# Linear attention with an MLP behind it: the products of queries with states move to the head of the next unit, and gated queries get two places

## The chip, the cores and the metric

The kernel runs on one core of a Trainium2 chip, all tensors in 32-bit floats. The metric is the device time of one execution in microseconds. Five runs of the kernel before took 703.0 to 706.71 us, with a median of 704.47. The execution that was profiled took 703.88 us.

## The reference

Four sequences of 768 tokens, with 8 heads of 48 channels. Each head carries a 48 x 48 state that is decayed by a gate f and grown by an outer product, and every token's query reads it. The result, as 3072 rows of 384 channels, goes through an MLP with 2048 hidden channels.

```
f = 1 / (1 + exp(-f_logit))                      # gate per token and channel
for t in range(768):
    state = f[t, :, None] * state + outer(k[t], v[t])
    y[t]  = q[t] @ state
x = y of all heads side by side                  # (3072, 384)
h = x @ w_in                                     # (3072, 2048)
out = (h * sigmoid(1.702 * h)) @ w_out           # (3072, 384)
```

## The kernel before

**Units and chunks.** The work is cut into 12 units of 256 tokens of one sequence (n = 0 to 11, three to a sequence), each with all heads. Two heads lie at partitions 0 and 64, four such pairs side by side along the free axis (`NP` = 4, `NA` = 1024 columns a plane). Inside a unit the sequence is handled in chunks of 64 tokens. Within a chunk the products of queries and keys are formed by halves: first neighbouring tokens, then pairs, then groups of 4, 8, 16 and 32 (`LEV`, six levels). At each level the keys and queries are multiplied by gate products (`promote`, L427), the scores are taken on TensorE (`score`, L384), masked out of PSUM by VectorE into `A` (`evacuate`, L408), and multiplied with the values into `y` in PSUM (`add`, L442). Across chunks a state is carried: VectorE multiplies the last state with a chunk's gate product and adds the chunk's key-value product (L561 to L566), and TensorE multiplies the queries with these states into the same `y` (L582).

**X.** The tile `X` has three planes of 1024 columns: plane 0 the queries, plane 1 the queries times the gate F (`begin_q`, L378), plane 2 the keys. Planes 1 and 2 are promoted in place. When all levels are done, plane 1 holds each query times all gates from its chunk's start, and L582 reads it there.

**Parts.** `attention(n)` yields a list of parts and five preparing functions. In the order in which they come for a unit with a successor from n = 3 on: W (first scores, 32 matmul records on L384, then promotion and masking); three V (two levels each: scores, products of the masked scores with values); B (`begin_f` and `begin` of the next unit: transposes of its gates and queries from `raw`, L331); two T (transposes of the keys on TensorE, L525, copied to `kn`); a second B, called K here (`begin_k` of the next unit: its keys' transpose into plane 2); S (last two `add`s, the key-value products on L546, the states on VectorE); W (the products with states, L582, the four copies of `y` to `yT` on ScalarE, L591, and six transfers that lay `yT` out as `xT`, L593 and L600; behind them, in the same part, `begin_q` and `begin_gates` of the next unit: one VectorE multiplication and six GpSimd multiplications of gates, L373).

**The MLP as filling.** The MLP of earlier units is a list of single matmuls, first layer (L620, 256 columns, three to a hidden block of 128) and second layer (L636, 384 columns, sixteen to a block of 128 rows). `merge` emits a part and then as many MLP matmuls as the part's share: W and S 3, V 4, B, T and K 1 each, 25 in all, for the 24,576 columns of one unit. So TensorE alternates between stretches of array-tile work (matmuls of 48 or 64 rows and columns, four at a time in quarters of the array) and blocks of full-size MLP matmuls. The list runs behind: when a unit's merge begins, 18 second-layer matmuls of an older unit (`LAG`) are still in it.

**Order.** TensorE's order is the order of emission throughout. The other engines follow the order of emission up to the end of unit 3 (`fill_order`); from unit 4 on their order is chosen by the scheduler of the framework from what is ready, earlier emitted work first. The weights arrive as two 16-bit halves each and are converted on VectorE in units 0 to 3.

**Buffers that the change touches.** `y`: one in PSUM (2 banks), taken by a unit's second part and free after its four copies. Scores `sc`: one, 2 banks. `kn` and `yT`: one buffer each, 4 KB a partition. `xT`: three. `st`: two.

Of the kernel before, what the change touches and what calls it, by code (L numbers as in the profile page):

```python
# [9 lines left out]
F32 = mybir.dt.float32  # L10
# [6 lines left out]
def view(t, offset, dims):  # L17

    a = t[:]
    return bass.AP(a.tensor, a.offset + offset, [list(a.ap[0])] + [list(d) for d in dims])  # L20
# [3 lines left out]
def kernel(  # L24
# [98 lines left out]

    F = const.tile([P, NA], F32, name="F")

    X = const.tile([P, 3, NA], F32, name="X")

# [181 lines left out]
    def rows(h):  # L311
        return slice(h * HS, h * HS + D)
# [5 lines left out]
    def attention(n):  # L318

        first = n % NU == 0
        t = {}
        parts = []

# [49 lines left out]
                off += nb  # L375

        def begin_q():
            nc.vector.tensor_tensor(X[:, 1], X[:, 0], F, ALU.mult)  # L378

        def score(out, lhs, rhs):  # L380

# [10 lines left out]
        def keys(l, tag="Kc"):  # L392
            return lambda h, x: t[tag, l][rows(h), x // 2:x // 2 + 64]
# [21 lines left out]
        def promote(l, q_too=False):  # L415

            m = LEV[l]
            nb = NA // (2 * m)  # L420
            qk = view(X, NA + m, [[NA - m, 2], [2 * m, nb], [1, m]])
            by = t["tms"][l].rearrange("p (n two) -> p two n", two=2).unsqueeze(3).broadcast_to((P, 2, nb, m))
            if n < N_FILL:
                nc.vector.tensor_tensor(qk[:, 1], qk[:, 1], by[:, 1], ALU.mult)
                nc.vector.tensor_tensor(qk[:, 0], qk[:, 0], by[:, 0], ALU.mult)
            else:
                nc.vector.tensor_tensor(qk, qk, by, ALU.mult)  # L427
            if l + 1 < NL:
                m = LEV[l + 1]
                for tag, j, hf in (("Kc", 2, 0), ("Qc", 1, 1))[:1 + q_too]:  # L430
                    c = t[tag, l + 1] = att.tile([P, NA // 2], F32, tag=tag, name=f"{tag}_{n}_{l}", bufs=2)
                    nc.scalar.copy(  # L432
                        c.rearrange("p (n m) -> p n m", m=m),
                        X[:, j].rearrange("p (n two m) -> p n two m", two=2, m=m)[:, :, hf, :],
                    )
# [17 lines left out]
        @part("W")  # L453
        def _():
            order_v(n + 1)
            sc = scores()
            score(
                sc.rearrange("p h (a t) -> p h a t", a=NP), lambda h, x: X[rows(h), 2, x:x + G:2],
                lambda h, x: view(X, x, [[NA + 1, 2], [2, 64]])[rows(h)],
            )  # L460
            promote(0)
            t["A"] = evacuate(512, [(0, 0)])

        @part("W" if n < N_FILL else "V")
        def _():
            sc = scores()
            s4 = sc.rearrange("p h (s a t) -> p s h a t", s=2, a=NP)
            score(s4[:, 0], lambda h, x: X[rows(h), 2, x + 1:x + G:2], lambda h, x: X[rows(h), 0, x + 1:x + G:2])
            score(s4[:, 1], keys(1), tokens(1, LEV[1], 1))
            A = t["A"]  # L470
            t["py"] = ps.tile([P, NG, NP, G], F32, tag="y", name=f"y_{n}")
            add(
                0, lambda h, g, a: A[g * 64:(g + 1) * 64, h, a * G:(a + 1) * G].rearrange("p (two n) -> p n two", two=2),
                lambda h, g, a: t["py"][columns(h, g), g, a, :], start=True,
            )
            if n < N_FILL:
                promote(1)
            else:
                promote(1, True)
                promote(2)  # L480
            t["A"] = evacuate(512, [(0, 0), (256, 1)])

        def level(l):
            sc = scores()
            score(sc[:, :, :256].rearrange("p h (a t) -> p h a t", a=NP), keys(l), tokens(1, LEV[l], 1))
            if l == 2:
                add(1, slot(t["A"], 0), half(1, 1))
                add(2, slot(t["A"], 256), half(LEV[1], 1))
            else:
                add(l, slot(t["A"], 0), half(LEV[l - 1], 1))  # L490
            if n + 1 >= N_TURN:
                for u in (0, 2) if l == 2 else (l,):
                    load_vl(n + 1, u)
            promote(l)
            t["A"] = evacuate(256, [(0, l)])

        def levels(l):

            s4 = scores().rearrange("p h (s a t) -> p s h a t", s=2, a=NP)
            score(s4[:, 0], keys(l), keys(l, "Qc"))  # L500
            score(s4[:, 1], keys(l + 1), tokens(1, LEV[l + 1], 1))
            for u, c in ((l - 1, 0), (l, 256)):
                add(u, slot(t["A"], c), half(LEV[max(u - 1, 0)], 1))
            for u in ((0, 2) if l == 2 else (l - 1, l)):
                load_vl(n + 1, u)
            promote(l + 1, l + 2 < NL)
            if l + 2 < NL:
                promote(l + 2)
            t["A"] = evacuate(512, [(0, l), (256, l + 1)])
# [7 lines left out]

        def turn_k(a0):
            if a0 == 0:
                t["kn"] = att.tile([P, NP, NG, P], F32, tag="kn", name=f"kn_{n}")  # L520
            pt = ps.tile([P, 2, NG, P], F32, tag="mm", name=f"tkn_{n}_{a0}", bufs=4)
            for a in range(2):
                for g in range(NG):
                    x = (a0 + a) * U + g * G
                    nc.tensor.transpose(pt[:, a, g, :], X[:, 2, x:x + G], ident)  # L525
            nc.scalar.copy(t["kn"][:, a0:a0 + 2], pt)
# [42 lines left out]
        @part("W")  # L569
        def _():  # L570

            py = t["py"]
            for cs in ((1, 2), (3, 0)):
                for a in range(NP):
                    for c in cs:
                        if t["before"][c] is None:
                            continue
                        for h in range(2):  # L580
                            x = a * U + c * C
                            nc.tensor.matmul(  # L582
                                py[columns(h, c // 2), c // 2, a, c % 2 * C:(c % 2 + 1) * C],
                                lhsT=t["before"][c][rows(h), a], rhs=X[rows(h), 1, x:x + C],
                                start=False, stop=True, skip_group_check=True,
                            )
            yT = att.tile([P, NP, NG, G], F32, tag="yT", name=f"yT_{n}")
            xT = xTs[n] = mlp.tile([P, NK, U], F32, tag="xT", name=f"xT_{n}", bufs=3)
            for g in range(NG):
                for h in range(2):  # L590
                    nc.scalar.copy(yT[rows(h), :, g, :], py[columns(h, g), g])  # L591
            for h in range(2):
                nc.sync.dma_start(  # L593
                    out=xT[h * D:(h + 1) * D].rearrange("p c (g t) -> p c g t", g=NG), in_=yT[rows(h), :NK]
                )
                at = 0
                while at < D:
                    c, p = (h * D + at) // DR, (h * D + at) % DR
                    w = min(D - at, DR - p)
                    nc.sync.dma_start(  # L600
                        out=xT[D2 + p:D2 + p + w, c].rearrange("p (g t) -> p g t", g=NG),
                        in_=yT[h * HS + at:h * HS + at + w, NK],
                    )
                    at += w
# [80 lines left out]

    def parts_of(n):

        parts = list(units[n][1])
        if n + 1 < NALL:
            begin_f, begin, begin_k, begin_gates, begin_q = units[n + 1][0]  # L690
            kind, fn = parts.pop()
            parts.append((kind, lambda: (fn(), begin_q(), begin_gates(), load_vl(n + 1, 0) if n + 1 < N_TURN else None)))


            i = len(parts)
            if n + 1 < N_FILL:
                parts.insert(i - 1, ("K", begin_k))
                parts.insert(i - 5, ("B", begin))
                parts.insert(i - 6, ("B", begin_f))
            else:  # L700
                parts.insert(i - 2, ("B", begin_k))
                parts.insert(i - 4, ("B", lambda: (begin_f(), begin())))
        if n < N_TURN:

            def with_v(part, *us):
                kind, fn = part
                return kind, lambda: (fn(), [load_vl(n, u) for u in us])
            levels = [i for i, (kind, _) in enumerate(parts) if kind == "W"][:NL]
            for i, us in zip(levels, [(0, 2) if n == 0 else (2,), (), (3,), (4,), (5,), (6,)]):
                parts[i] = with_v(parts[i], *us)  # L710
        return parts
# [93 lines left out]
```

## Time and profile before

| what | us |
|---|---|
| median of 5 runs | 704.47 (703.0 to 706.71) |
| the profiled execution | 703.88 |
| its span, first to last instruction | 702.0 |
| MLP matmuls, first layer L620 (1152 records), busy | 262.2 |
| MLP matmuls, second layer L636 (768 records), busy | 261.7 |
| products with values L442 (2688 records), busy | 57.1 |
| scores L384 (1344 + 768 + 576 records in three groups), busy | 28.4 + 22.7 + 12.5 |
| products with states L582 (704 records), busy | 13.8 |
| period of a unit from unit 7 to unit 8 (start of first scores, 431.94 to 485.66) | 53.72 |

A 32-bit matmul leaves two records. Busy times on TensorE overlap where four quarter-array matmuls run at once, so they are no shares of the time. The columns of the chain of waits are start, length, and what ran; of a timeline they are start, length, engine, line, operation, output and inputs, shapes, count, and in brackets the idle time before and what ended it.

### The profile page before, as it was taken

The numbers are of one execution on the slowest core, as the hardware profiler recorded it, in microseconds if no ns is written. First come the engines' busy times: TensorE is split into PE (matmuls) and PEld (weight loads), VectorE is DVE, ScalarE is ACT, GpSimd is POOL, SyncE is SP. The second block draws the span as 40 slices with busy tenths as digits, with TensorE's granted clock in tenths as the row PEclk, the third lists the DMA queues.
The fourth block names the chain that finished last, engine by engine and source line by source line (L and its number), as shares of the span: only waits on it lengthen the run. The fifth ranks groups of instructions, "written<-read, shape, count | busy, mean of one in ns | idle before, by whom it ended". The sixth has DMA issues, their size and how long they took to land.

```text
span 702.0 us, 20695 instructions
## 1 busy us (share of the span) xinstructions
PE 679.3 (97%) x9208; PEld 506.7 (72%) x9208; DVE 395.5 (56%) x683; ACT 211.4 (30%) x440; POOL 39.8 (6%) x90
## 2 busy tenths in 40 slices
PE   6779989999999999999999999999999999999998
PEld 5656767767867886886786785786786786786774
DVE  3999787987666644644644644654654644441120
ACT  4454433324123222322322322322331332232110
POOL 3020100010010000001001001001001001000000
PEclk9999999999999999999999999999999999999999
DMA  8867963581082534325325314415404102001000
GB/s 204 217 160 194 222 166 103 152 181 37 23 198 79 157 76 114 92 77 126 99 68 123 111 54 118 131 41 129 133 24 123 47 25 80 13 2 36 11 1 22
DMA packets 66897, 69.66 MB, mean 99 GB/s; under 512 B 29944, under 2 KB 59256, under 8 KB 66808
## 3 DMA queue, kind: packets, MB, share of 16 engines
q1 hardware_dynamic: 66808, 68.34, 38.0%
q8 instruction: 72, 1.18, 0.7%
q14 instruction: 17, 0.14, 0.1%
HBM read 58.88 MB, written 8.65 MB: 96 GB/s over the span
## 4 chain that ended last, share of the span: by engine, by line
PE 89%; DVE 4%; DMA 3%; SPq 1%; issue 1%; ACT 0%; DVEq 0%; ACTq 0%
PE o L636 36%; PE h L620 35%; PE sc L384 7%; PE y L442 6%; PE y L582 2%; PE sc L546 1%; PE tkn L525 1%; DMA bits<-in_moe_w_in_dram 1%; DMA raw<-in_q_dram 1%; DMA bits<-in_moe_w_out_dram 1%; SPq L244 1%; DVE s L209 1%; SPq L170 1%; PE t L343 1%; DVE A L408 0%
## 5 line engine op out<-in xcount | busy, mean ns | idle before, releaser
L636 PE MATMUL o<-w_out,g 128*128 128x384 f32 x768 | 261.7, 492 | 2.2 <-DVE g L626 2.2
L620 PE MATMUL h<-xT,w_in 128*128 128x256 f32 x1152 | 262.2, 382 | 0.2 <-DVE g L626 0.2
L620 PEld LDWEIGHTS h<-xT,w_in 128*128 128x128 f32 x1152 | 214.8, 190 | 34.7 <-issue 2.1
L636 PEld LDWEIGHTS o<-w_out,g 128*128 128x128 f32 x768 | 142.2, 190 | 96.6 <-issue 5.0
L626 DVE TENSOR_TENSOR g<-h,sg 128x256 f32<-128x256 f32 x192 | 80.5, 422 | 145.5 <-ACT sg L625 145.1
L625 ACT ACTIVATE sg<-h 128x256 f32<-128x256 f32 x192 | 73.1, 383 | 175.1 <-PE h L620 172.3
L432 ACT COPY Kc<-X 128x512 f32<-128x512 f32 x60 | 37.7, 629 | 125.3 <-DVE X L427 96.6
L427 DVE TENSOR_TENSOR X<-X,tot 128x1024 f32<-128x1024 f32 x45 | 55.0, 1221 | 21.1 <-PE sc L384 17.8
L408 DVE TENSOR_TENSOR A<-sc,masks 128x512 f32<-128x512 f32 (+1 forms) x84 | 61.1, 755 | 0.0
L442 PE MATMUL y<-A,vl 64*48 64x64 f32 (+1 forms) x2688 | 57.1, 230 | 1.9 <-issue 1.9
L442 PEld LDWEIGHTS y<-A,vl 64*48 64x48 f32 x2688 | 48.9, 121 | 7.6 <-issue 7.1
L591 ACT COPY yT<-y 48x512 f32<-48x512 f32 x48 | 27.8, 580 | 70.6 <-PE y L582 69.4
L373 POOL TENSOR_TENSOR tot<-F 128x512 f32<-128x512 f32 x12 | 12.5, 1039 | 542.6 <-DVE st L563 485.7
L331 DVE STREAM_TRANSPOSE X<-raw 128x1024 f32<-128x1024 f32 x18 | 36.9, 2051 | 10.8 <-PE sc L384 10.2
L378 DVE TENSOR_TENSOR X<-X,F 128x1024 f32<-128x1024 f32 x12 | 15.4, 1284 | 29.3 <-PE y L582 21.2
L384 PEld LDWEIGHTS sc<-X 48*64 48x64 f32 x768 | 18.1, 138 | 18.3 <-issue 14.9
L384 PE MATMUL sc<-X,Kc 48*64 48x64 f32 x1344 | 28.4, 222 | 2.4 <-DVE A L408 2.4
L427 DVE TENSOR_TENSOR X<-X,F 128x1024 f32<-128x1024 f32 x9 | 11.0, 1226 | 33.2 <-PE sc L384 33.2
L384 PEld LDWEIGHTS sc<-X,Kc 48*64 48x64 f32 x1344 | 24.3, 136 | 7.2 <-issue 3.2
L384 PE MATMUL sc<-X 48*64 48x128 f32 (+1 forms) x768 | 22.7, 255 | 5.9 <-DVE A L408 4.6
L343 PE MATMUL t<-ident,raw 128*64 128x128 f32 x288 | 19.9, 299 | 5.7 <-DMA raw<-in_f_logit_dram 4.4
L373 POOL TENSOR_TENSOR tot<-tot 128x256 f32<-128x256 f32 (+4 forms) x60 | 25.0, 417 | 4.7
(52 smaller groups left out, 375.6 us busy)
## 6 DMA issues: line engine op xcount, KB each, us to landing
vl<-v_tok SPq DMA_DIRECT2D x50, 192.0 KB, 3.1
bits<-in_moe_w_out_dram SPq DMA_DIRECT2D x8, 768.0 KB, 8.6
bits<-in_moe_w_in_dram SPq DMA_DIRECT2D x8, 576.0 KB, 6.5
v_tok<-in_v_dram SPq DMA_DIRECT2D x10, 384.0 KB, 6.4
vl<-v_tok SPq DMA_DIRECT2D x10, 384.0 KB
vn<-v_tok SPq DMA_DIRECT2D x10, 384.0 KB, 6.7
xT<-yT SPq DMA_DIRECT2D x24, 144.0 KB, 2.6
raw<-in_f_logit_dram SPq DMA_DIRECT2D x18, 192.0 KB, 3.9
```

The lines of the kernel that those rows point to most:

```text
L331: nc.vector.transpose(out.rearrange("p (a i j) -> p a j i", a=NP, j=R), raw[:, j].rearrange("p a (j d) -> p (a j) d", j=R)[:, :, :32],)
L373: nc.gpsimd.tensor_tensor(tn, t2[:, :, 0], t2[:, :, 1], ALU.mult)
L384: nc.tensor.matmul(out[g * HS:(g + 1) * HS, h, a, :], lhsT=lhs(h, a * U + g * G), rhs=rhs(h, a * U + g * G), start=True, stop=True,)
L408: nc.vector.tensor_tensor(A[:, :, c:c + w].rearrange("p h (x t) -> p h x t", t=64), t["sc"][:, :, c:c + w].rearrange("p h (x t) -> p h x t ...
L427: nc.vector.tensor_tensor(qk, qk, by, ALU.mult)
L432: nc.scalar.copy(c.rearrange("p (n m) -> p n m", m=m), X[:, j].rearrange("p (n two m) -> p n two m", two=2, m=m)[:, :, hf, :],)
L442: nc.tensor.matmul(dst(h, g, a), lhsT=vls[n, u][g * 64:(g + 1) * 64, (2 * a + h) * D:(2 * a + h + 1) * D], rhs=A(h, g, a), start=(start an ...
L591: nc.scalar.copy(yT[rows(h), :, g, :], py[columns(h, g), g])
L620: nc.tensor.matmul(ph, lhsT=w_in[:, c, ff * P:(ff + 1) * P], rhs=xTs[n][:, c, :], start=(c == 0), stop=(c == NK - 1))
L625: nc.scalar.activation(sg, ph, AF.Sigmoid, scale=1.702)
L626: nc.vector.tensor_tensor(g[ff // FG][:, ff % FG, :], ph, sg, ALU.mult)
L636: nc.tensor.matmul(t["po"], lhsT=g[ff // FG][:, ff % FG, tt * P:(tt + 1) * P], rhs=w_out[:, ff, :], start=(ff == ffs[0]), stop=(ff == ffs[ ...
```

## The change

From the unit after the fill on, the last part of a unit (the products with states and all that follows them) is no longer a part of its own. It is emitted at the head of the next unit's first part, just ahead of that unit's first scores. This holds for the products of units 3 to 10; those of units 0 to 2 and of unit 11 stay parts of their own. `begin_q` and `begin_gates` of the next unit come behind the states (part S) in these units. As a unit's products are now read after the next unit's gated queries are written, `X` has a fourth plane, and units from 3 on use plane 3 and plane 1 in turn (`J`). `kn` and `yT`, which are not in use at the same time, share one buffer.

```diff
-    X = const.tile([P, 3, NA], F32, name="X")
+    X = const.tile([P, 4, NA], F32, name="X")
...
+        J = 1 if n < N_FILL or (n - N_FILL) % 2 else 3
...
         def begin_q():
-            nc.vector.tensor_tensor(X[:, 1], X[:, 0], F, ALU.mult)
+            nc.vector.tensor_tensor(X[:, J], X[:, 0], F, ALU.mult)
...
-            qk = view(X, NA + m, [[NA - m, 2], [2 * m, nb], [1, m]])
+            qk = view(X, J * NA + m, [[(2 - J) * NA - m, 2], [2 * m, nb], [1, m]])
...
-                lambda h, x: view(X, x, [[NA + 1, 2], [2, 64]])[rows(h)],
+                lambda h, x: view(X, x, [[J * NA + 1, 2], [2, 64]])[rows(h)],
...
-                t["kn"] = att.tile([P, NP, NG, P], F32, tag="kn", name=f"kn_{n}")
+                t["kn"] = att.tile([P, NP, NG, P], F32, tag="kn", name=f"kn_{n}", bufs=1)
...
-                                lhsT=t["before"][c][rows(h), a], rhs=X[rows(h), 1, x:x + C],
+                                lhsT=t["before"][c][rows(h), a], rhs=X[rows(h), J, x:x + C],
...
-            yT = att.tile([P, NP, NG, G], F32, tag="yT", name=f"yT_{n}")
+            yT = att.tile([P, NP, NG, G], F32, tag="kn", name=f"yT_{n}", bufs=1)
...
         parts = list(units[n][1])
+        if n > N_FILL:
+            kind, scores = parts[0]
+            _, inter = units[n - 1][1][-1]
+            parts[0] = kind, lambda: (inter(), scores())
         if n + 1 < NALL:
             begin_f, begin, begin_k, begin_gates, begin_q = units[n + 1][0]
             kind, fn = parts.pop()
-            parts.append((kind, lambda: (fn(), begin_q(), begin_gates(), load_vl(n + 1, 0) if n + 1 < N_TURN else None)))
             i = len(parts)
             if n + 1 < N_FILL:
-                parts.insert(i - 1, ("K", begin_k))
-                parts.insert(i - 5, ("B", begin))
-                parts.insert(i - 6, ("B", begin_f))
+                parts.insert(i, ("K", begin_k))
+                parts.insert(i - 4, ("B", begin))
+                parts.insert(i - 5, ("B", begin_f))
             else:
-                parts.insert(i - 2, ("B", begin_k))
-                parts.insert(i - 4, ("B", lambda: (begin_f(), begin())))
+                parts.insert(i - 1, ("B", begin_k))
+                parts.insert(i - 3, ("B", lambda: (begin_f(), begin())))
+            if n < N_FILL:
+                parts.append((kind, lambda: (fn(), begin_q(), begin_gates(), load_vl(n + 1, 0) if n + 1 < N_TURN else None)))
+            else:
+                state_kind, states = parts.pop()
+                parts.append((state_kind, lambda: (states(), begin_q(), begin_gates())))
```

The other places of plane 1 (the tokens of a level's scores and the copies `Qc`) become plane J in the same way. The positions at which the transposes of the next unit are inserted are the same as before, counted from a list that lacks the last part. From unit 3 to unit 10 a unit's shares sum to 22 in place of 25; unit 11 has 23 in both.

More of the change, by code (lines that the diff above doesn't have):

```diff
@@ L429, in promote @@
                 m = LEV[l + 1]
-                for tag, j, hf in (("Kc", 2, 0), ("Qc", 1, 1))[:1 + q_too]:
+                for tag, j, hf in (("Kc", 2, 0), ("Qc", J, 1))[:1 + q_too]:
                     c = t[tag, l + 1] = att.tile([P, NA // 2], F32, tag=tag, name=f"{tag}_{n}_{l}", bufs=2)
@@ L468, in _ @@
             score(s4[:, 0], lambda h, x: X[rows(h), 2, x + 1:x + G:2], lambda h, x: X[rows(h), 0, x + 1:x + G:2])
-            score(s4[:, 1], keys(1), tokens(1, LEV[1], 1))
+            score(s4[:, 1], keys(1), tokens(J, LEV[1], 1))
             A = t["A"]
@@ L484, in level @@
             sc = scores()
-            score(sc[:, :, :256].rearrange("p h (a t) -> p h a t", a=NP), keys(l), tokens(1, LEV[l], 1))
+            score(sc[:, :, :256].rearrange("p h (a t) -> p h a t", a=NP), keys(l), tokens(J, LEV[l], 1))
             if l == 2:
@@ L500, in levels @@
             score(s4[:, 0], keys(l), keys(l, "Qc"))
-            score(s4[:, 1], keys(l + 1), tokens(1, LEV[l + 1], 1))
+            score(s4[:, 1], keys(l + 1), tokens(J, LEV[l + 1], 1))
             for u, c in ((l - 1, 0), (l, 256)):
```

## The prediction

> **What bounds the kernel.** I read three views in this order: the page's busy and clock rows, TensorE's list of waits, the chain of waits piece by piece over one steady unit.
>
> ```profile
> PE 679.3 (97%) x9208; PEld 506.7 (72%) x9208; DVE 395.5 (56%) x683; ACT 211.4 (30%) x440; POOL 39.8 (6%) x90
> PEclk9999999999999999999999999999999999999999
> PE 89%; DVE 4%; DMA 3%; SPq 1%; issue 1%; ACT 0%; DVEq 0%; ACTq 0%
> ```
>
> TensorE is busy 97% of the span at full clock, and 89% of the chain lies on it. A busy share is an average, so the next question is where it waits. Asked from 98 us to the end, TensorE's waits have one line:
>
> ```profile
> PE tkn L525 <- ACT kn L526: 0.7, 1, 0.7
> ```
>
> One wait of 0.7 us in 604 us. From 98 us on the time is simply TensorE's own work, one piece after another; no other engine decides, and nothing that only hurries VectorE, ScalarE or a transfer can gain. The change begins after that point (unit 3's products are at 208 us). So it can gain only what it takes off TensorE's own sequence, and lose only by a new wait. The sequence around units 6 to 8, from the chain (start us, length us, what):
>
> ```profile
> 426.19 1.04 PE y L582 x64
> 427.23 4.71 PE o L636 x14
> 431.94 1.08 PE sc L384 x32
> 433.02 5.36 PE o L636 x16
> 438.38 1.11 PE sc L384 x62
> ...
> 447.27 1.09 PE sc L384 x64
> 448.36 0.90 PE y L442 x64
> 449.25 7.10 PE h L620 x32
> ...
> 472.58 1.04 PE y L442 x64
> 473.63 0.92 PE sc L546 x64
> ...
> 677.83 20.65 PE o L636 x64
> ```
>
> Two prices are in it. **The boundary**: at the kernel's tail 64 second-layer records without interruption take 20.65 us, 0.3227 each. Sixteen between two stretches of array-tile work should take 5.16 and take 5.36: 0.20 more. First-layer blocks say the same: 96 in the tail take 20.72 (0.2158 each), so 32 should take 6.91 and take 7.10. Each block between two stretches pays 0.195 us. **The entry**: 64 y records take 1.04 us where they open a stretch, 0.90 where they follow scores in it: 0.14 us for being first.
>
> **The change, part by part.**
>
> *Merging.* Before, a unit's TensorE order ends S (states), MLP, W (y with states, L582), MLP, then the next unit's first scores (L384 x32), MLP. After, L582 and those scores stand together. It happens for the products of units 3 to 10: 8 times (unit 2's still stand alone, unit 11 has no successor). Nothing is computed less: the 64 records of L582, the 32 of L384 and the MLP matmuls (24,576 columns a unit) remain. What goes is one MLP block between stretches, its matmuls joining others: 0.195 us, and one entry, up to 0.14. The junction of 48x48 tiles with 48x64 tiles is not in the trace. Nearest rows: y after scores (448.36) takes 0.90, the entry wholly saved: 0.335 a merge. If the scores pay a full entry again, 0.195 is saved; if the junction cost an entry and a boundary, nothing. Shapes also change inside the stretches at 448.36 and 473.63 with 64 records in 0.90 and 0.92, so I take the good end, 0.33: 8 x 0.33 = 2.6 us. Ends: 0 and 8 x 0.335 = 2.7; with a full entry 8 x 0.195 = 1.6.
>
> *Shares.* The W part's 3 shares go, so a unit's MLP columns are spread over 22 shares, not 25 (unit 11 keeps its 23). A column costs 0.645 us / 384 = 1.68 ns, so three shares rise from 4.95 to 5.63 us and four from 6.6 to 7.5. This is cover, not time: it widens every gap in which VectorE and ScalarE prepare the next stretch. One gap disappears, and these are the places where a wait could appear:
>
> *States to products.* VectorE's state instructions of the S part:
>
> ```profile
> 474.62 0.35 DVE L566 TENSOR_TENSOR st<-st,sc 128x192 f32<-128x192 f32 x1 [1.80 <-PE sc L546]
> ...
> 476.96 0.35 DVE L566 TENSOR_TENSOR st<-st,sc 128x192 f32<-128x192 f32 x1
> ```
>
> S ends at 474.5, the states at 477.3: 2.8 us, against 5.6 of MLP. Slack 2.8.
>
> *Gated queries (L378), one VectorE instruction of 1.23 us.* Before it waited for L582, because it overwrote the plane that L582 reads ("DVE X <- PE y L582", 21.2 us in all), off the path. With a second plane that wait goes. Emitted right behind the states, it ends 2.8 + 1.23 = 4.1 us after S; the scores need it at 5.6 + 1.04 = 6.7. Price nothing, slack 2.6; without that cover, 1.23 a unit. (VectorE may also take it earlier, as soon as the new queries are transposed, at 441; then it is further from the path still.) Behind it on VectorE stand g multiplications of 0.42 us, at this place of the unit second-layer time without any. The six gate products on POOL (1.04 + 2.09 us) start, as before, when the states have read the old ones.
>
> The Trainium skill's SBUF — State Buffer page (Terms, "shared port pair") speaks against this: a VectorE instruction with two SBUF inputs and a GpSimd instruction that reads SBUF lock each other out for a whole instruction. L378 and the gate products now fall together, which no row before shows. By the rule L378 could start one product (1.04 us) later and end 5.1 us after S instead of 4.1, still ahead of 6.7: the sum is the same by both.
>
> *L582's followers.* Four ScalarE copies (2.37 us), six SP transfers, then the first layer of that unit:
>
> ```profile
> 427.31 2.37 ACT L591 COPY yT<-y 48x512 f32<-48x512 f32 x4 [8.66 <-PE y L582]
> 434.34 0.67 ACT L432 COPY Kc<-X 128x512 f32<-128x512 f32 x1 [1.89 <-DVE X L427]
> ```
>
> The copies must free the single y buffer before the next y: formerly 12 us later (439.3), now 1.08 + 5.63 + 1.1 = 7.8 us, needed 2.5. Kc comes a VectorE instruction after the scores (1.23) and now has these copies before it on ScalarE: ready some 2.1 us after the scores, used after 5.6. SP issued the six transfers until 434.7, 7.6 us after L582; with 2.6 to land, 10.2. The first layer that reads them starts after 18 second-layer matmuls (6,912 columns): 1.08 + 5.63 + 3.2 for the next stretch + 5.98 = 15.9 us. Slack 5.7. On SP the order for a later unit's v (L264, issued at 428.64) stood ahead of these six and now stands behind them in the program; its readers were issued 20 us later (448.9), so neither place costs.
>
> *yT in kn's buffer.* yT is written after kn's last reader (S), kn some 25 us after yT's transfers began: nothing. *X with a fourth plane*: the same instructions at another stride (for half the units a negative one), 1.23 us each before; no row prices such a stride, VectorE's slack covers a doubling of the first (promotion, 1.23 more against some 3.5 until Kc is read). *Unit 3's part list* has 22 shares too, with weight conversion ending one part earlier: 8 conversions a V part instead of 6 or 7, at most 1.1 us more VectorE work (0.55 each) in a gap grown by 1.2. Nothing.
>
> **Sum.** The profiled execution took 703.88 (span 702.0, 1.9 around it): 703.88 - 2.6 = 701.2. It lies 0.6 below the median shown, 704.47, so on the median 701.8.
>
> **Rivals.**
>
> *1. The junction costs what the boundary did, or all but the 0.195.* For it: the opening matmuls of both stretches pay 0.14 and the scores bring new tile widths. Against: shape changes at 448.36 and 473.63 cost 0.02 at most. Time 702.9 to 704.5.
>
> *2. Slower: the scores wait in the merged stretch for L378.* Before, MLP stood between L582 and the scores and hid L378's 1.23 us; now only L582's 1.04 does after the states are needed. If L378 lands on VectorE behind something that itself waits for L582 (the next unit's first state product, L563, stood next to it at 428.45), the scores wait for 0.36 + 1.23 and two hand-overs of 0.14 (S's end at 474.48 in TensorE's records to 474.62): 1.9 us, 8 times, less the 2.6 gained: 704.47 + 15.2 - 2.6 = 717. It decides as soon as L378 ends more than 6.7 us after S; each us beyond costs 8, so the gain is gone at 7.0. For it: from unit 4 on only TensorE's order is written by hand, VectorE's is chosen. Against: L378 precedes that L563 in the program and no longer waits for TensorE.
>
> *3. First-layer matmuls wait for xT.* It needs 5.7 us more delay on SP; 2 us beyond would cost 16: 718. Nothing in SP's list is that long.
>
> **How the numbers follow.** Forecast 0.65, rival 1 0.23, rivals 2 and 3 together 0.12. About 0.3% (2.1 us) is what this measurement tells from no change. The forecast's 2.6 is only just over it: of 0.65 some 0.07 falls within by scatter, of rival 1 some 0.04 beyond, giving 0.62 faster; within 0.26; slower 0.12. The forecast's own range is 700.4 (703.0, the lowest run, less 2.6) to 703. For 8 in 10 it must take in rival 1 up to 704.5 and some scatter: 700.3 to 704.8, leaving out rivals 2 and 3.
>
> **What would show it.** The chain from 260 us on should have L582 x64 directly followed by L384 x32, together about 2.0 us, with no second-layer piece between; a unit's period 53.72 us (431.94 to 485.66) should fall to about 53.4; TensorE's list of waits should stay empty. Wrong if that list shows L384 behind VectorE X L378, L442 behind ScalarE yT, or L620 behind the xT transfers; or if L582 and L384 together take 2.3 or more.

## The result, and the profile after

| | before | after |
|---|---|---|
| median of the runs, us | 704.54 (53 runs, 702.03 to 707.71) | 702.29 (27 runs, 699.95 to 705.7) |
| the profiled execution's span, us | 702.0 | 697.8 |
| period of a steady unit, us | 53.72 | 53.34 |
| from the first key-value product (S) of unit 2 to TensorE's last record, us | 561.9 | 559.7 |

The ratio of the times is 0.9967, 95% interval 0.9957 to 0.9977: 2.3 us less, between 1.6 and 3.0. The two spans differ by more, 4.2 us, but 2.0 of that lies ahead of unit 2's states (136.09 before, 134.12 after), in units whose order of work the change leaves as it was. One difference there is the clock: the profiled execution before went through a short stretch of lower clock and the one after did not. The windows view, from 50 to 56 us, first before, then after; the last three columns are the granted clock, the share of the DMA engines and GB/s:

```profile
50.00:56.00 6.00, 5.36 (x104) 4.73 (x104) 5.84 (x13) 1.57 (x4) 0.00 (x0) 0.72 1.04 265
```

```profile
50.00:56.00 6.00, 5.41 (x184) 4.55 (x183) 6.00 (x14) 1.00 (x2) 0.00 (x0) 1.00 1.01 220
```

So spans of single executions aren't compared below. The table's last row leaves that stage out and is used instead.

The changed file's lines stand three further down: products with states L585, scores L387, gated queries L381, first layer L623, second layer L639. The page's busy row, and TensorE's waits from 98 us on, after the change:

```profile
PE 674.4 (97%) x9208; PEld 504.7 (72%) x9208; DVE 396.7 (57%) x683; ACT 211.8 (30%) x440; POOL 40.7 (6%) x90
```

```profile
PE tkn L528 <- ACT kn L529: 0.7, 1, 0.7
PE h L623 <- DVE g L629: 0.6, 1, 0.6
```

The first wait is the old one; the second is new. The chain of waits over a steady unit (start, length, what):

```profile
422.60 5.36 PE o L639 x16
427.95 1.04 PE y L585 x64
428.99 0.92 PE sc L387 x31
429.91 6.00 PE o L639 x18
435.92 1.12 PE sc L387 x64
```

The products and the scores now stand together, 1.96 us, where they were 1.04 and 1.08 with a block of 14 second-layer records between. The scores have lost 0.16 of their 1.08: as the second of a stretch they pay no entry.

Both signs of the change can be read in the table. The period fell by 0.38 us a unit, which over 8 merges is 3.0, while the long stretch fell by 2.2. Some 0.8 was given back at one place. TensorE's records show it in unit 3, right behind the states, as VectorE's timeline (first fence) and GpSimd's (second) of the changed kernel say:

```profile
207.80 0.35 DVE L569 TENSOR_TENSOR st<-st,sc 128x192 f32<-128x192 f32 x1
208.07 1.98 DVE L381 TENSOR_TENSOR X<-X,F 128x1024 f32<-128x1024 f32 x1
209.98 0.74 DVE L629 TENSOR_TENSOR g<-h,sg 128x256 f32<-128x256 f32 x2
```

```profile
207.94 1.04 POOL L376 TENSOR_TENSOR tot<-F 128x512 f32<-128x512 f32 x1 [65.72 <-DVE st L566]
209.06 2.95 POOL L376 TENSOR_TENSOR tot<-tot 128x256 f32<-128x256 f32 x5
```

L381 took 1.98 us instead of 1.23, five gate products on GpSimd 2.95 instead of 2.08, and a g multiplication that first-layer matmuls were waiting for came only at 209.98. TensorE resumed at 210.45, 0.78 us later than its records' even spacing would have it.

### The profile page after: what moved, and what is told of

It is laid out like the page before. It is cut to its first block, busy times and chain, and to the rows that moved or that the text cites. A ratio compares the mean times of both kernels' runs of the same rounds, so it can differ in the third digit from the quotient of the medians.

```text
span 697.8 us, 20710 instructions
## 1 busy us (share of the span) xinstructions
PE 674.4 (97%) x9208; PEld 504.7 (72%) x9208; DVE 396.7 (57%) x683; ACT 211.8 (30%) x440; POOL 40.7 (6%) x90
## 4 chain that ended last, share of the span: by engine, by line
PE 92%; DVE 4%; DMA 2%; issue 2%; ACT 1%; SPq 0%; DVEq 0%; ACTq 0%
PE o L639 36%; PE h L623 35%; PE sc L387 7%; PE y L445 6%; PE t L346 2%; PE y L585 2%; PE sc L549 1%; PE tkn L528 1%; DMA bits<-in_moe_w_in_dram 1%; PE tv L280 1%; DVE A L411 1%; DMA raw<-in_q_dram 0%; DVE s L211 0%; DVE st L569 0%; DVE st L566 0%
## 5 line engine op out<-in xcount | busy, mean ns | idle before, releaser
L639 PE MATMUL o<-w_out,g 128*128 128x384 f32 x768 | 260.7, 491 | 2.3 <-DVE g L629 2.3
L623 PE MATMUL h<-xT,w_in 128*128 128x256 f32 x1152 | 261.5, 382 | 0.8 <-DVE g L629 0.8
L623 PEld LDWEIGHTS h<-xT,w_in 128*128 128x128 f32 x1152 | 215.3, 190 | 35.8 <-issue 2.0
L639 PEld LDWEIGHTS o<-w_out,g 128*128 128x128 f32 x768 | 142.4, 190 | 96.0 <-issue 5.0
L376 POOL TENSOR_TENSOR tot<-F 128x512 f32<-128x512 f32 x12 | 12.5, 1039 | 542.4 <-DVE st L566 485.8
L658 ACT COPY osb<-o 128x384 f32<-128x384 f32 x18 | 8.6, 478 | 108.8 <-PE o L639 108.7
L594 ACT COPY yT<-y 48x512 f32<-48x512 f32 x48 | 27.8, 580 | 15.1 <-PE y L585 14.5
L387 PE MATMUL sc<-X,Kc 48*64 48x64 f32 x1344 | 28.0, 220 | 2.6 <-DVE A L411 2.4
L387 PEld LDWEIGHTS sc<-X,Kc 48*64 48x64 f32 x1344 | 23.9, 134 | 7.4 <-issue 2.7
L569 DVE TENSOR_TENSOR st<-st,sc 128x192 f32<-128x192 f32 x44 | 15.6, 354 | 22.6 <-PE sc L549 21.2
L387 PEld LDWEIGHTS sc<-X 48*64 48x64 f32 x768 | 18.2, 134 | 13.2 <-issue 11.7
L566 DVE TENSOR_TENSOR st<-st,tot 128x192 f32<-128x192 f32 x44 | 15.7, 357 | 20.8 <-PE y L585 11.9
L387 PE MATMUL sc<-X 48*64 48x128 f32 (+1 forms) x768 | 22.5, 250 | 4.9 <-DVE A L411 4.2
```

The costliest lines, as they stand in the source:

```text
L376: nc.gpsimd.tensor_tensor(tn, t2[:, :, 0], t2[:, :, 1], ALU.mult)
L387: nc.tensor.matmul(out[g * HS:(g + 1) * HS, h, a, :], lhsT=lhs(h, a * U + g * G), rhs=rhs(h, a * U + g * G), start=True, stop=True,)
L623: nc.tensor.matmul(ph, lhsT=w_in[:, c, ff * P:(ff + 1) * P], rhs=xTs[n][:, c, :], start=(c == 0), stop=(c == NK - 1))
L639: nc.tensor.matmul(t["po"], lhsT=g[ff // FG][:, ff % FG, tt * P:(tt + 1) * P], rhs=w_out[:, ff, :], start=(ff == ffs[0]), stop=(ff == ffs[ ...
```

## The experiments

Each kernel differs from the changed one by the edit shown. The last column of the table is the stretch from unit 2's S to TensorE's last record (559.7 after the change); each ratio is to the kernel before, on the same chip.

| kernel | ratio (95%) | period, us | stretch, us |
|---|---|---|---|
| one MLP matmul between | 1.0005 (0.9987 to 1.0023) | 54.33 | 562.4 |
| parts apart, two planes | 0.9997 (0.9979 to 1.0014) | 53.72 | 561.9 |
| scores first | 0.9972 (0.9954 to 0.9989) | 53.37 | 559.9 |
| one plane | 1.0155 (1.0133 to 1.0177) | 54.90 | 574.8 |
| early gated queries in unit 3 | 0.994 (0.992 to 0.996) | 53.34 | 558.8 |
| late gates for unit 4 | 0.9961 (0.9942 to 0.998) | 53.34 | 559.7 |
| gates held until L381 is done | 0.9953 (0.9939 to 0.9968) | 53.34 | 558.9 |
| unit 2 merged too | 0.9978 (0.9963 to 0.9993) | 53.34 | not comparable, S of unit 2 moves |

**One MLP matmul between the two halves of a merge.** It separates the joining itself from everything else that the change brought.

```diff
-            parts[0] = kind, lambda: (inter(), scores())
+            parts[0] = kind, lambda: (inter(), between(), scores())
...
+    def between():
+        w, emit, _ = fill.pop(0)
+        emit()
```

> One MLP matmul of the filling is emitted between the products with states and the next unit's scores, 8 times; everything else as after the change. Theory (a merge saves one block boundary and one entry of array-tile work, 0.36 us): each merge is undone by that single matmul, the unit period goes back from 53.34 to about 53.7 us and the time rises by 8 x 0.36 = 2.9 us over the changed kernel, to about 705.2, slightly over the kernel before because the 0.8 us stall in unit 3 stays. Rival (the gain comes from the larger shares or the second plane): period 53.34 and about 702.3, as after the change.

The gain is gone. The long stretch rose by 2.76 us, 0.345 a merge. The shares (22 a unit), the plane and the shared buffer are those of the changed kernel, so none of these makes the gain. The chain shows the whole price of one matmul in the wrong place:

```profile
434.62 1.04 PE y L585 x64
435.66 0.84 PE o L639 x2
436.50 1.08 PE sc L387 x32
```

Two records that take 0.65 in a block take 0.84 between two stretches, and the scores are back at 1.08: 0.19 + 0.16 = 0.35. The expected period of 53.7 was missed for a reason of bookkeeping: the matmul comes on top of the unit's share, so a unit holds 0.645 us more MLP (54.33 - 0.645 = 53.69) and the tail that much less.

**Parts apart, two planes.** The other half of that test: everything but the merge.

```diff
-        if n > N_FILL:
-            kind, scores = parts[0]
-            _, inter = units[n - 1][1][-1]
-            parts[0] = kind, lambda: (inter(), scores())
...
                 parts.append((state_kind, lambda: (states(), begin_q(), begin_gates())))
+                parts.append((kind, fn))
```

> The fourth plane, the shared buffer and the gated queries behind the states stay; the products with states are a part of their own again, as before the change. Theory (only the merge gains; the plane takes off a wait of VectorE that lay on no path): the unit period is 53.72 us as before the change, and the time that of the kernel before, ratio 1.000 (0.999 to 1.002, the upper end if unit 3 stalls here too). Rival (the plane gains by itself): period nearer 53.34, ratio 0.997.

Period 53.72 and stretch 561.9, to the hundredth the kernel before. The plane, the shared buffer and the earlier gated queries gain nothing, though L381 no longer waits for TensorE in the steady units. There is no wait for g in unit 3 either, although L381 is as long there as in the changed kernel:

```profile
206.58 1.99 DVE L381 TENSOR_TENSOR X<-X,F 128x1024 f32<-128x1024 f32 x1
```

With 25 shares, what follows that S on TensorE begins with second-layer matmuls, as before the change.

**Scores first, products behind them.**

```diff
-            parts[0] = kind, lambda: (inter(), scores())
+            parts[0] = kind, lambda: (scores(), inter())
```

> In the merged stretch the scores of the next unit come first and the products with states behind them; all else as after the change. Theory (a stretch pays one entry, whoever opens it, and nothing at the joint of 48x64 and 48x48 tiles): the merged stretch adds 2.1 to 2.2 us to the MLP's time as in the changed kernel (2.155), the period stays 53.34 within 0.05, the time 702.3. Rival 1 (the joint has a price of its own, which the one order hides and the other doesn't): over 2.25 us a stretch, period 53.45 or more, 1 us or more on the time.

The merged stretch as the chain has it:

```profile
430.66 1.08 PE sc L387 x32
431.75 0.89 PE y L585 x64
432.64 6.00 PE o L639 x18
```

Now the scores pay the entry and the products don't: 1.97 together against 1.96. By the spacing of TensorE's records a stretch adds 2.16 to 2.17 us in this order, 2.15 to 2.16 in the other (one of the eight 2.18), and the long stretches differ by 0.17 us in eight joints. The joint of different tile shapes costs some 0.02 at most; rival 1 falls.

**One plane.** The price that the second plane avoids.

```diff
-            parts[0] = kind, lambda: (inter(), scores())
+            begin_gated = units[n][0][4]
+            parts[0] = kind, lambda: (inter(), begin_gated(), scores())
...
-                parts.append((state_kind, lambda: (states(), begin_q(), begin_gates())))
+                parts.append((state_kind, lambda: (states(), begin_gates())))
...
-        J = 1 if n < N_FILL or (n - N_FILL) % 2 else 3
+        J = 1
```

> The merge with one plane of gated queries: L381 stands between the products with states, which read the plane, and the scores, which need it. Theory (rival 2's price): TensorE waits in each merged stretch for L381, 1.23 us and two hand-overs of 0.14 to 0.2, about 1.5 us; a unit's period 53.34 + 1.5 = 54.8, and 8 x 1.5 = 12 less the 0.8 that unit 3's stall no longer costs: about 713 to 714. Rival (the second plane is not needed, the scores' wait is covered): about 702.

TensorE's list of waits has the line that rival 2 spoke of, eight times:

```profile
PE sc L387 <- DVE X L381: 10.8, 8, 1.4
```

The period rose by 1.56 us as expected, 12.5 in all, less the 0.8 in unit 3. But the stretch rose by 15.1. The remaining 3.4 us is not a wait. The windows view of this kernel (the granted clock is third from the end):

```profile
262.00:273.00 11.00, 9.64 (x223) 6.59 (x226) 3.99 (x9) 2.06 (x4) 2.82 (x6) 1.00 0.57 156
273.00:278.40 5.40, 5.40 (x38) 3.07 (x31) 4.30 (x3) 1.58 (x4) 0.00 (x0) 0.68 0.70 141
...
604.00:609.50 5.50, 5.50 (x41) 3.27 (x36) 2.37 (x3) 1.57 (x3) 0.00 (x0) 0.69 0.31 73
```

Twice, shortly after a merged stretch with its wait, the granted clock drops; the records show half clock for 3.4 us each time, and second-layer records there come every 0.64 us instead of 0.32. Two such windows cost 3.4 us. So the second plane gains nothing by itself, as the parts apart have shown, but without it the merge loses time.

**Early gated queries in unit 3.** The first of three on the 0.8 us that was lost.

```diff
-                parts.insert(i - 1, ("B", begin_k))
+                parts.insert(i - 1, ("B", (lambda: (begin_q(), begin_k())) if n == N_FILL else begin_k))
...
-                parts.append((state_kind, lambda: (states(), begin_q(), begin_gates())))
+                parts.append((state_kind, lambda: (states(), n == N_FILL or begin_q(), begin_gates())))
```

> In unit 3 alone the gated queries of unit 4 (L381) are formed ahead of the keys' transpose, not behind the states. Theory (in unit 3, where VectorE's order is the order of emission, L381 holds up the g multiplications behind the states, and first-layer matmuls run out of PSUM buffers): the one TensorE wait for g after 98 us, 0.6 to 0.8 us at about 210 us, is gone, about 701.5. Rival (the g multiplications wait for the states or for ScalarE, not for L381): the wait stays, 702.3.

The wait for g is gone from the list and the stretch is 0.9 us shorter. Moved there, L381 has its usual length:

```profile
206.86 1.22 DVE L381 TENSOR_TENSOR X<-X,F 128x1024 f32<-128x1024 f32 x1
```

That is the same instruction on the same plane, so neither the plane nor its stride made it 1.98. The run leaves open whether L381's place alone made the wait or its extra length did.

**Late gates for unit 4** was meant to tell, by taking GpSimd's work away from beside L381.

```diff
-                parts.append((state_kind, lambda: (states(), begin_q(), begin_gates())))
+                parts.append((state_kind, lambda: (states(), begin_q(), n == N_FILL or begin_gates())))
...
-            parts[0] = kind, lambda: (inter(), scores())
+            late = units[n][0][3] if n == N_FILL + 1 else tuple
+            parts[0] = kind, lambda: (late(), inter(), scores())
```

> L381 stays behind the states of unit 3, but the six gate products of unit 4 on GpSimd move to the head of the next unit, so nothing on GpSimd runs beside L381. Theory (L381 took 1.98 us there, 0.75 more than elsewhere, because GpSimd's gate products ran beside it): L381 takes 1.23 again, and the wait of TensorE for g at about 210 us shrinks from 0.78 to under 0.1, about 701.6. Rival (L381 is slow there for another reason, such as the plane's stride): 1.98 and 0.78 stay, 702.3.

The edit did not do what it was for, and the run decides nothing between the two. GpSimd has nothing else to do at that time and waits only for the old gate products to have been read, so the instructions, though emitted later, started at the same point: L381 1.99 us, the five products 2.95, the wait unchanged. Emitting the products later did not hold them back, since neither other work of GpSimd nor data stood ahead of them.

**Gates held until L381 is done** uses data: a copy of one column of L381's output on GpSimd, ahead of the gate products.

```diff
+    def hold():
+        one = att.tile([P, 1], F32, tag="one", name="one")
+        nc.gpsimd.tensor_copy(one, X[:, 1, :1])
...
-                parts.append((state_kind, lambda: (states(), begin_q(), begin_gates())))
+                parts.append((state_kind, lambda: (states(), begin_q(), hold() if n == N_FILL else None, begin_gates())))
```

> In unit 3 a one-column copy on GpSimd that reads L381's output stands ahead of the gate products, so that these start only when L381 is done; VectorE's order is that of the changed kernel. Theory (L381's 1.98 us are 1.23 and 0.75 of GpSimd's first gate product beside it): L381 takes 1.23, GpSimd's five later products 2.08 instead of 2.95, and TensorE's wait for g at about 210 us falls from 0.78 to under 0.1, about 701.6. Rival (the length comes from VectorE's place behind the states): L381 keeps 1.98 and the wait 0.78, 702.3.

VectorE's timeline, then GpSimd's:

```profile
209.77 0.35 DVE L569 TENSOR_TENSOR st<-st,sc 128x192 f32<-128x192 f32 x1
210.04 1.22 DVE L381 TENSOR_TENSOR X<-X,F 128x1024 f32<-128x1024 f32 x1
211.18 0.75 DVE L629 TENSOR_TENSOR g<-h,sg 128x256 f32<-128x256 f32 x2
```

```profile
211.32 0.19 POOL L691 COPY one<-X 128x1 f32<-128x1 f32 x1 [67.13 <-DVE X L381]
211.46 1.04 POOL L376 TENSOR_TENSOR tot<-F 128x512 f32<-128x512 f32 x1
212.58 2.07 POOL L376 TENSOR_TENSOR tot<-tot 128x256 f32<-128x256 f32 x5
```

Same place behind the states, 1.22 us, no wait of TensorE for g, and the stretch is 0.8 us shorter. So it was not L381's place that cost: its 1.22 us fit into the cover. The 0.76 us that it lost beside GpSimd's products did not fit.

**Unit 2 merged too**, with the gated queries ahead of the keys' transpose in every unit from 2 on.

```diff
-        if n > N_FILL:
+        if n >= N_FILL:
...
-                parts.insert(i - 1, ("B", begin_k))
+                parts.insert(i - 1, ("B", (lambda: (begin_q(), begin_k()))))
...
-            if n < N_FILL:
+            if n < N_FILL - 1:
...
-                parts.append((state_kind, lambda: (states(), begin_q(), begin_gates())))
+                parts.append((state_kind, lambda: (states(), begin_gates())))
```

> The changed kernel with the gated queries formed ahead of the keys' transpose in every unit from 2 on, and with the products of unit 2 merged into unit 3 as well (9 merges). Theory: against the changed kernel 0.8 us (the stall in unit 3, as when it was taken away alone) and 0.36 us (a ninth merge) less, 1.2 us; ratio to the kernel before about 0.995; no wait of TensorE for g near 210 us; period 53.34. Rival (in units 2 and 3, where every engine follows the order of emission, the larger shares and the earlier states turn into new waits): the 0.36 is not to be seen, or a wait for g appears at about 140 us.

The ninth merge works (2.15 us for the joined stretch at 149 us) but the rival came true, with other waits than the one it named:

```profile
PE tkn L528 <- ACT kn L529: 1.3, 1, 1.3
PE h L623 <- DMA xT<-yT: 0.6, 1, 0.6
```

The transposes of unit 2's keys wait 0.6 us longer, and unit 2's first layer waits for its own input: it follows only 8 second-layer matmuls (16 records) after the products, where in the changed kernel it follows 15, as the products now come one MLP block later. The records show 0.8 us for this wait. Together about 1.4 against 0.36. The traces agree: from unit 1's first key-value product to TensorE's last record this kernel takes 617.1 us and the one with early gated queries in unit 3 alone 616.0, both with one stretch of 3.4 us at half clock in it. That one has the lowest ratio of all, 0.994 (0.992 to 0.996) of the kernel before; its interval overlaps those of the changed kernel and of the one with the gates held, so the times alone do not rank these three. The stretches put it and the one with the gates held 0.9 and 0.8 us ahead of the changed kernel.

## Why the prediction was right, and which step failed

The direction, the size and the mechanism held: 701.8 was forecast, 702.29 was measured. Two errors stand behind that, 0.2 to 0.3 us too little gain from the merges and 0.8 us lost in unit 3, and they offset each other in part; that the total came so near is partly luck.

*Merging.* Right. The boundary and the entry were 0.195 and up to 0.14; I took 0.33 a merge. By the records' spacing the two stretches added 1.238 + 1.281 us to the MLP and the joined one adds 2.155: 0.364. Putting one matmul between gives 0.345 back. The term of 2.6 measured 2.8 to 2.9. It was a little short because the scores' entry is 0.16, not 0.14.

*Shares and planes as cover, not time.* Right in the steady units: the kernel with the parts apart (two planes, 25 shares) is equal to the one before to 0.01 us in period and in the long stretch, and the one with a matmul between (two planes, 22 shares) has no gain left. In unit 3 the shares did cost, as said below.

*States to products, followers of L582, yT in kn's buffer.* Right for the steady units: TensorE's list has no wait from them. ScalarE's four copies did come to stand before `Kc`, as said; they ended at 431.5 and `Kc` followed at once, done 3.7 us ahead of the stretch that reads it.

*Gated queries.* Right for units from 4 on: VectorE took L381 at 442, after the new queries were transposed and with 1.3 us of idle time behind it, far from the path. In unit 3, still ordered by hand, it was left behind the states.

*Unit 3's part list: "Nothing."* Wrong: 0.8 us. I counted the weight conversions and did not carry over to this unit what I had said of the others, that the MLP behind S is second-layer work with no g to wait for. With 22 shares unit 3's S is followed by first-layer matmuls, which need a g for every buffer in PSUM that they take. It took both, these matmuls and a long L381: with the parts apart L381 had 1.99 us and there was no wait for g, with the gates held 22 shares and no such wait either.

*The rule on the shared port.* The case which the prediction set beside its sum is the one that happened, in unit 3. Side by side, L381 took 1.98 us and the five products 2.95; apart they took 1.22 and 2.07. The Trainium skill's SBUF — State Buffer page (section "SBUF: two separate sides") has a VectorE instruction with two SBUF inputs and a GpSimd instruction that reads SBUF exclude each other for a whole instruction, with the one that starts first keeping the ports. The trace agrees: the first gate product, which began 0.13 us before L381, kept its 1.04 us, L381 ended 1.07 us after it (0.15 less than its own length), and the five products behind it took 0.88 us longer. The prediction said that no row before shows the two together. That was wrong; the kernel before has them in its first units, here VectorE's row, then GpSimd's:

```profile
43.48 1.93 DVE L378 TENSOR_TENSOR X<-X,F 128x1024 f32<-128x1024 f32 x1
```

```profile
43.30 1.04 POOL L373 TENSOR_TENSOR tot<-F 128x512 f32<-128x512 f32 x1 [30.33 <-DVE st L563]
44.41 3.33 POOL L373 TENSOR_TENSOR tot<-tot 128x256 f32<-128x256 f32 x5
```

There TensorE's scores waited 0.7 us for L378. So this price could have been read before the change was run. As the prediction had it, L381 still ended long before the scores needed it. I set its cost at nothing by comparing the delay with the scores' time alone, and not with that of the g multiplications queued behind L381.

*Rival 2* was sized at 1.9 us a unit for an L381 behind another instruction; with L381 alone between, the wait is 1.35 (10.8 in 8), and the clock adds to it what no sum of waits has in it.

## What to carry to other kernels

When one engine has no waits, count its changes of mode: here each return from quarter-array matmuls to full ones and back costs about 0.35 us beside the work itself, and joining two stretches that are both ready saves that, whatever their order. Before joining, look for what was computed under the block that disappears, and give it a second buffer; then check the unit at the edge of the schedule, where the order rules differ, with its own list of what follows what. Work on GpSimd that is "off the path" was not free here: beside it a VectorE instruction with two SBUF inputs took 1.98 us instead of 1.22, and others waited behind that.

## What the runs showed of the hardware

A TensorE wait of 1.4 us in the midst of a stretch may cost more than itself: in the kernel with one plane, two of eight such waits were followed within 2 us by 3.4 us at half clock, 1.7 us lost each. In the nine other profiled executions, in which TensorE waits at most twice after 110 us (1.3 us the longest), no such window lies between there and the end of TensorE's work. That speaks for the waits as the cause but does not show it: it is one execution with two windows, and why two waits of eight and not all is open.

Windows of half clock, of the same length or twice it, appear in the first 110 us of the profiled executions, in a number that differs between executions (one before the change, none after, one to three in the others). They are one source of the scatter between runs of the same kernel: of the changed kernel's 27 runs, 699.95 to 705.7 us, the two with the lowest mean granted clock (0.989 and 0.99) are the two longest (705.7 and 704.89), and the two at 1.000 took 701.06 and 700.84.
